# Down projection of a GeGLU feed-forward: product M2 moved between the groups of a half, and W21 loaded once per half

## The chip, the cores and the metric

The kernel runs on one core of a Trainium2 chip. The metric is the device time of one execution in microseconds (us), as the median over several runs. A core has a matrix engine (TensorE, "PE" in the profile, with its weight loads as "PEld"), three engines for elementwise work (VectorE or DVE, ScalarE or ACT, GpSimd or POOL), and SyncE (SP), which here issues most of the DMAs. The engines run side by side, each works through its own instructions in order, and they wait for each other on semaphores. TensorE writes its results to PSUM, eight banks of 128 x 512 f32, numbered 0 to 7.

## What is computed

```python
# x: (1, 2048, 1024), w_gate and w_up: (1024, 3584), w_down: (3584, 1024), all bf16
def reference(x, w_gate, w_up, w_down):
    return (_gelu(x @ w_gate) * (x @ w_up)) @ w_down
```

## The kernel before

The 2048 tokens are done in two halves (`h`) of 1024. For each half a gate/up part makes the hidden values `hT` (features on the partitions), and a down part multiplies them by `w_down`. The change lies in the down part, and this section tells of that.

**The seven products.** The down part works on two groups (`grp`) of 512 tokens per half, in `down_group`. In each group the product is split two by two, into blocks of 256 tokens, 1792 features and 512 output columns, and Strassen's scheme in Winograd's form makes it out of seven block products in place of eight. With A for the hidden values and W for `w_down`:

- S1 = A21 + A22, S2 = S1 - A11, S3 = A11 - A21, S4 = A12 - S2
- T1 = W12 - W11, T2 = W22 - T1, T3 = W22 - W12, T4 = W21 - T2
- M1 = A11 W11, M2 = A12 W21, M3 = S4 W22, M4 = A22 T4, M5 = S1 T1, M6 = S2 T2, M7 = S3 T3
- C11 = M1 + M2, C22 = M1 + M6 + M7 + M5, C12 = M1 + M6 + M5 + M3, C21 = M1 + M6 + M7 + M4

M1 and M2 take bf16 operands as they are. The other five take sums, kept in f32 form (`s_mem` for S and the copy of A22, `t_mem` for T and the copy of W22). A product is 14 steps (`NS`, 128 features each) for each of two sets of 128 tokens (`u`), so 28 matmuls of 128 x 512, which `product` issues in a list's order.

**The banks.** Each product has a pair of banks, one for each `u`. M1 goes to PB and is copied to QB by ScalarE (L781). M5 goes to VB and is copied out to `m5` (L802). M6 is added to QB, which is then copied to RB (L817), and `add_m5` adds M5 to QB on VectorE (L742). M7 is added to RB, and a second `add_m5` writes RB + M5 to VB, which is C22. M2 is added to PB (C11), M3 to QB (C12), M4 to RB (C21). `evacuate` (L766 and L768, in halves L757 and L759) casts finished banks to bf16 in `o_sb` buffers, of which there are four, and `store` (L774) sends them out from SyncE. PB, VB, QB and RB are the pairs (0, 1), (2, 3), (4, 5), (6, 7).

**The order.** It is written out by hand: `pe`, `dve`, `act` and `sp` chain an engine's instructions in the order in which the program issues them. In a group it is M1, M5, M6, M7, M2, M3, M4. The `behind_...` functions put the work for later products between the matmuls of the running one: S by `s_down` on VectorE (L675; the copy of A22 on ScalarE, L667), T1 and T3 by `t_down` on VectorE (L605), the copy of W22 on ScalarE (L602), T2 and T4 by DMA from a DRAM buffer, `t_dram`, that the first half's gate/up part filled (L600). `t_mem` is a ring of 20 blocks for five sequences of 14, so a T load waits for the matmuls that read the block before. In the first half, X for the next half is loaded from DRAM during the first group's M6 and M7 (L973, behind `x_fill`).

**W21.** `load_b21` (L569) loads it in four tiles: three of 512 KB into `wd_sb` buffers, of which there are three, and the last of 256 KB into an `o_sb` buffer. Each group issues all four behind M6. In a half's first group one of the three `wd_sb` buffers still holds a part of S3 that M7 reads.

Of the kernel before, what the change touches and what calls it, by code (L numbers as in the profile page):

```python
# [34 lines left out]
def kernel(  # L35
# [33 lines left out]
    NS = KF // 2  # L69
    NR = 20  # L70
    NGRP = SH // TB
# [35 lines left out]
    PB, VB, QB, RB = (0, 1), (2, 3), (4, 5), (6, 7)  # L107
# [11 lines left out]
    def sp(inst):  # L119
        return on("sp", inst)  # L120

    def act(inst):
        return on("act", inst)

    def dve(inst):
        return on("dve", inst)
# [12 lines left out]
    def pe(inst):  # L139
        return on("pe", inst)  # L140
# [414 lines left out]


    BPT = WDT * D // DN
    b21_tiles = {}

    def load_b21(n, q):  # L560
        i0, i1 = q * BPT, min((q + 1) * BPT, NS)
        if i1 < NS:
            w = wd_pool.tile([P, WDT, D], BF16, name="wd_sb")
            w = w[:].rearrange("p a d -> p (a d)")
        else:
            w = o_pool.tile([P, (i1 - i0) * DN], BF16, name="o_sb")[:]
        w = w.rearrange("p (b n) -> p b n", n=DN)
        src = wdv[:, NS + i0 : NS + i1, 0:DN]
        sp(nc.sync.dma_start(out=w[:, 0 : i1 - i0, :], in_=src))  # L569
        b21_tiles[(n, q)] = w  # L570

    def right(grp, name, i0, i1):

# [18 lines left out]
    def t_down(grp, name, i0, i1):  # L592

        for i in range(i0, i1, 2):
            t = right(grp, name, i, i + 2)
            rows = wd_rows(i, i + 2)
            b11, b12 = rows[:, :, 0:DN], rows[:, :, DN:D]
            if name in ("t2", "t4"):
                src = t_dram[:, i : i + 2, 0 if name == "t2" else 1, :]
                sp(nc.sync.dma_start(out=t.bitcast(F32), in_=src))  # L600
            elif name == "b22":
                act(nc.scalar.copy(out=t, in_=b22_blocks(i, i + 2)))  # L602
            else:
                in0, in1 = (b12, b11) if name == "t1" else (b22_blocks(i, i + 2), b12)
                dve(nc.vector.tensor_tensor(out=t, in0=in0, in1=in1, op=ALU.subtract))  # L605
# [51 lines left out]
    def s_down(hT, grp, name, i0, i1):  # L657
        n = 0 if name in ("s1", "s2", "s4") else 1
        for i in range(i0, i1, 2):
            t = s3_early(i) if (grp, name) == (0, "s3") and i < 4 else left(n, i, i + 2)  # L660

            def a(l, j):
                c0 = grp * TB + l * 2 * P
                return hT[:, j * NS + i : j * NS + i + 2, c0 : c0 + 2 * P]

            if name == "a22":
                act(nc.scalar.copy(out=t, in_=a(1, 1)))  # L667
                continue
            in0, in1, op = {
                "s1": lambda: (a(1, 0), a(1, 1), ALU.add),  # L670
                "s2": lambda: (t.bitcast(F32), a(0, 0), ALU.subtract),
                "s3": lambda: (a(0, 0), a(1, 0), ALU.subtract),
                "s4": lambda: (a(0, 1), t.bitcast(F32), ALU.subtract),
            }[name]()
            dve(nc.vector.tensor_tensor(out=t, in0=in0, in1=in1, op=op))  # L675
# [2 lines left out]
    NSPLIT = 4  # L678
    DH = DN // 2

    def down_group(hT, h, grp, then):
        last_grp = h == NH - 1 and grp == NGRP - 1
        more = grp + 1 < NGRP
        t0 = grp * TB
        n = h * NGRP + grp

        def done(name):
            for f in then.get(name, ()):
                f()
# [7 lines left out]
        def product(name, bset, lhs, rhs, start, stop, behind=None, order=plain):  # L697

            left_of = [0] * NS
            for i, u, *part in order:  # L700
                bank, c0, c1 = part or (bset[u], 0, DN)
                pe(
                    nc.tensor.matmul(  # L703
                        banks[bank][:, c0:c1],
                        lhsT=lhs(i, u),
                        rhs=rhs(i)[:, c0:c1],
                        start=start and i == 0,
                        stop=stop and i == NS - 1,
                        skip_group_check=True,
                    )  # L710
                )
                left_of[i] += 1
                if behind is not None and left_of[i] == 2 and i % 2 == 1:
                    behind(i - 1)

        def h_block(l, j):
            def lhs(i, u):
                c0 = t0 + (2 * l + u) * P
                return hT[:, j * NS + i, c0 : c0 + P]

            return lhs

        def lsum(n):
            return lambda i, u: left(n, i, i + 1)[:, 0, u * P : (u + 1) * P]
# [6 lines left out]
        def rsum(name):  # L731
            return lambda i: right(grp, name, i, i + 1)[:, 0, :]
# [2 lines left out]
            return wd_rows(i, i + 1)[:, 0, 0:DN]  # L735

        def b21(i):
            return b21_tiles[(h * NGRP + grp, i // BPT)][:, i % BPT, :]

        def add_m5(dst, src, u):  # L740
            dve(
# [5 lines left out]
        def evacuate(bset, l, d, halves=False):  # L747

            outs = []
            for u in range(2):  # L750
                if halves and u == 1:
                    r0 = h * SH + t0 + (2 * l + u) * P
                    for bank, c in ((bset[u], 0), (VB[u], DH)):
                        dst = o_pool.tile([P, DN], BF16, name="o_sb")[:, 0:DH]
                        src = banks[bank][:, c : c + DH]
                        if c == 0:
                            dve(nc.vector.tensor_copy(out=dst, in_=src))  # L757
                        else:
                            act(nc.scalar.copy(out=dst, in_=src))  # L759
                        c0 = d * DN + c  # L760
                        outs.append((out2[r0 : r0 + P, c0 : c0 + DH], dst))
                    continue
                dst = o_pool.tile([P, DN], BF16, name="o_sb")[:]
                r0 = h * SH + t0 + (2 * l + u) * P
                if last_grp and u == 0:
                    dve(nc.vector.tensor_copy(out=dst, in_=banks[bset[u]][:]))  # L766
                else:
                    act(nc.scalar.copy(out=dst, in_=banks[bset[u]][:]))  # L768
                outs.append((out2[r0 : r0 + P, d * DN : (d + 1) * DN], dst))
            return outs  # L770

        def store(outs):
            for dst, src in outs:
                sp(nc.sync.dma_start(out=dst, in_=src))  # L774

        def store_last(dst, src):
            act(nc.scalar.dma_start(out=dst, in_=src))

        product("m1", PB, h_block(0, 0), b11, True, False)
        for u in range(2):  # L780
            act(nc.scalar.copy(out=banks[QB[u]][:], in_=banks[PB[u]][:]))  # L781
        done("m1")

        def behind_m5(i):

            s_down(hT, grp, "s2", i, i + 2)
            if NT2 + i < NS:
                t_down(grp, "t2", NT2 + i, NT2 + i + 2)
            elif more:
                late.append(i + NT2 - NS)  # L790
            else:
                t_down(grp, "t3", i + NT2 - NS, i + NT2 - NS + 2)
# [12 lines left out]
        def behind_m6(i):  # L805
            if NT2 + i < NS:
                t_down(grp, "t3", NT2 + i, NT2 + i + 2)
            else:
                s_down(hT, grp, "s4", i + NT2 - NS, i + NT2 - NS + 2)
            if i == 4:  # L810
                for q in range(4):
                    load_b21(n, q)

        product("m6", QB, lsum(0), rsum("t2"), False, False, behind_m6, tail)
        s_down(hT, grp, "s4", NT2, NS)
        for u in range(2):
# [14 lines left out]
        s_down(hT, grp, "a22", 0, NS)  # L831
        out22 = evacuate(VB, 1, 1)
        done("m7")
        store(out22)
        product("m2", PB, h_block(0, 1), b21, False, True)
        out11 = evacuate(PB, 0, 0)
        done("m2")


# [6 lines left out]
                    t_down(grp + 1, "t1", NT2 + i - NS, NT2 + i - NS + 2)  # L846

        product("m3", QB, lsum(0), rsum("b22"), False, True, behind_m3)
        store(out11 + evacuate(QB, 0, 1))
        done("m3")  # L850

        def behind_m4(i):
            if not more:
                return
            if NT2 + i < NS:
                t_down(grp + 1, "t1", NT2 + i, NT2 + i + 2)
            else:
                t_down(grp + 1, "t2", NT2 + i - NS, NT2 + i - NS + 2)
# [23 lines left out]
    for h in range(NH):  # L882
# [9 lines left out]
        for pair in range(first_pair, NPAIR):  # L892
# [14 lines left out]
            if h == 0 and pair >= PPG:  # L907

                n = [min(4 * (pair - PPG + d), NSTEP) for d in range(3)]
# [16 lines left out]
            if 6 < pair < 11:  # L926
                i = 2 * pair - 8
# [81 lines left out]
        for grp, then in enumerate((then0, then1)):  # L1009
            down_group(hT, h, grp, then)  # L1010
# [30 lines left out]
```

## Time and profile before

| | |
|---|---|
| time of 3 runs, median | 539.78 us |
| lowest and highest | 539.51 and 540.17 us |
| span of the profiled execution, first to last instruction | 538.0 us |
| granted TensorE clock over the span | 1.000 |
| down groups within the span | 183.2 to 271.3 us, 447.0 to 535.1 us |
| DMA: moved, mean rate | 102.70 MB, 191 GB/s |

The profile is of one execution, whose own time is told by its span; the runs' times are of executions without a profile and hold some 1.8 us around the span as well. Busy times are of instructions, without waits. A row of the timeline has the start in us from the span's start, the length in us, the engine, the line of the kernel, the operation, out<-in, and how many instructions it merges; what stands in brackets is the engine's idle time before it and what ended it. Some matmul records are missing from the trace, so a product of 28 shows 27 at times. Rows of DMA queues (SPq) show the issue alone; the time to the landing is asked for by tile or line.

### The profile page before, as it was taken

How to read it: one execution, taken by the hardware profiler on the slowest of the kernel's cores; microseconds unless marked ns; L12 is line 12 of the kernel's file. 1: busy time of each engine (PE TensorE's matmuls, PEld its weight loads, DVE VectorE, ACT ScalarE, POOL GpSimd, SP SyncE). 2: the span in 40 equal slices, each digit the busy share in tenths (PEclk: the TensorE clock that was granted, in tenths of full speed). 3: DMA queues.
4: the chain of work that ended last, by engine and by line, in shares of the span. 5: the costliest groups of instructions: out<-in, count | busy, mean ns of one | idle time of the engine just before them, and what ended most of it. 6: DMA issues, size and time to landing. Idle time of an engine off the chain costs nothing.

```text
span 538.0 us, 7084 instructions
## 1 busy us (share of the span) xinstructions
PE 532.4 (99%) x2352; PEld 377.9 (70%) x2388; DVE 364.2 (68%) x476; ACT 263.5 (49%) x447; POOL 244.4 (45%) x212
## 2 busy tenths in 40 slices
PE   9999999999999999999999999999999999999997
PEld 4577776666776686777776677777777766866866
DVE  1988777788775997989574334444444469969861
ACT  2555555555555329117465555555555552462280
POOL 0699877777776000000056776666777730000000
PEclk9999999999999999999999999999999999999999
DMA  9946876785815977789950405041322448677846
GB/s 205 323 128 195 207 252 185 238 262 197 291 61 200 361 239 246 237 279 308 324 171 1 156 1 158 15 142 57 100 78 80 155 133 284 220 246 252 293 141 212
DMA packets 92547, 102.70 MB, mean 191 GB/s; under 512 B 18656, under 2 KB 67424, under 8 KB 92512
## 3 DMA queue, kind: packets, MB, share of 16 engines
q1 hardware_dynamic: 69568, 80.23, 46.0%
q10 hardware_dynamic: 22944, 22.02, 13.4%
q8 instruction: 19, 0.31, 0.2%
q14 instruction: 16, 0.13, 0.1%
HBM read 85.98 MB, written 12.58 MB: 183 GB/s over the span
## 4 chain that ended last, share of the span: by engine, by line
PE 99%; issue 0%; ACT 0%; ACTq 0%
PE bank L413 63%; PE bank L703 33%; PE bank L264 3%; PE bank L202 1%; PE bank L308 0%; ACT bank L468 0%; ACT o_sb L759 0%; ACTq L468 0%
## 5 line engine op out<-in xcount | busy, mean ns | idle before, releaser
L413 PE MATMUL bank<-t_mem,s_mem 128*128 128x512 f32 x1056 | 249.6, 394 | 0.0
L413 PEld LDWEIGHTS bank<-t_mem,s_mem 128*128 128x128 f32 x1056 | 198.1, 188 | 44.1 <-DVE bank L436 0.4
L385 POOL TENSOR_TENSOR s_mem<-w_mem 128x512 fp32r<-128x512 bf16 x102 | 120.3, 1201 | 190.7 <-DVE t_mem L259 102.8
L703 PE MATMUL bank<-t_mem,s_mem 128*128 128x512 f32 (+1 forms) x548 | 127.2, 391 | 0.0
L288 DVE TENSOR_TENSOR hT<-w_mem,bank 128x512 bf16<-128x512 f32 x104 | 71.3, 687 | 79.9 <-PE bank L413 45.7
L703 PEld LDWEIGHTS bank<-t_mem,s_mem 128*128 128x128 f32 x548 | 102.4, 188 | 22.1 <-issue 0.2
L436 DVE TENSOR_TENSOR bank<-bank,m 128x512 f32<-128x512 f32 x108 | 69.9, 694 | 45.2 <-ACT m L458 43.7
L413 PE MATMUL bank<-xT,w_mem 128*128 128x512 bf16 x405 | 96.5, 380 | 1.4
L283 ACT ACTIVATE w_mem<-bank 128x512 f32<-128x512 f32 x104 | 61.8, 596 | 52.9 <-DVE bank L436 35.8
L413 PEld LDWEIGHTS <-w_mem 128*128 128x128 bf16 x432 | 40.2, 98 | 51.6 <-issue 6.8
L385 POOL TENSOR_TENSOR s_mem<-w_mem,s_mem 128x512 fp32r<-128x512 bf16 x52 | 65.8, 1285 | 0.0
L605 DVE TENSOR_TENSOR t_mem<-w_mem 128x1024 fp32r<-128x1024 bf16 x56 | 65.6, 1219 | 0.0
L385 POOL TENSOR_TENSOR s_mem<-s_mem,w_mem 128x512 fp32r<-128x512 f32 x52 | 60.9, 1192 | 0.0
L464 ACT COPY bank<-bank 128x512 f32<-128x512 f32 x54 | 30.8, 570 | 38.9 <-PE bank L413 38.9
L398 ACT CAST s_mem<-w_mem 128x512 fp32r<-128x512 bf16 x54 | 33.1, 615 | 30.6 <-PE bank L413 29.1
L675 DVE TENSOR_TENSOR s_mem<-hT 128x512 fp32r<-128x512 bf16 x52 | 34.2, 686 | 10.2 <-PE bank L703 9.4
L458 ACT COPY m<-bank 128x512 f32<-128x512 f32 x54 | 31.8, 589 | 17.5 <-PE bank L413 17.5
L703 PEld LDWEIGHTS <-hT 128*128 128x128 bf16 x224 | 21.3, 98 | 26.6 <-issue 2.1
L468 ACT COPY bank<-bank 128x512 f32<-128x512 f32 x54 | 30.7, 570 | 12.7 <-PE bank L413 12.7
L630 DVE TENSOR_TENSOR o_sb<-wd_sb,o_sb 128x512 fp32r<-128x512 bf16 x28 | 31.5, 1126 | 0.5
L768 ACT CAST o_sb<-bank 128x512 bf16<-128x512 f32 x27 | 14.8, 585 | 33.9 <-PE bank L703 33.9
L602 ACT CAST t_mem<-w_mem 128x1024 fp32r<-128x1024 bf16 x28 | 26.9, 1048 | 0.0
(45 smaller groups left out, 238.6 us busy)
## 6 DMA issues: line engine op xcount, KB each, us to landing
t_mem<-t_dram SPq DMA_DIRECT2D x56, 512.0 KB, 5.2
w_mem<-in_w_gate_dram ACTq DMA_DIRECT2D x10, 1024.0 KB, 5.5
w_mem<-in_w_up_dram ACTq DMA_DIRECT2D x10, 1024.0 KB, 5.5
wd_sb<-in_w_down_dram SPq DMA_DIRECT2D x28, 256.0 KB, 4.5
t_dram<-o_sb SPq DMA_DIRECT2D x28, 256.0 KB, 2.4
wd_sb<-in_w_down_dram SPq DMA_DIRECT2D x12, 512.0 KB, 7.7
w_mem<-in_w_down_dram SPq DMA_DIRECT2D x4, 1024.0 KB, 6.6
w_mem<-in_w_down_dram SPq DMA_DIRECT2D x8, 512.0 KB, 8.3
```

What stands on the lines that cost most here:

```text
L283: act(nc.scalar.activation(out=g_sb, in_=ps[:], func=ACT.Gelu_apprx_tanh))
L288: nc.vector.tensor_tensor(out=hT[:, fc, tb * TB : (tb + 1) * TB], in0=g_sb, in1=ps[:], op=ALU.mult,)
L385: pool(nc.gpsimd.tensor_tensor(out=t, in0=in0, in1=in1, op=op))
L398: act(nc.scalar.copy(out=t, in_=a(1, 1)))
L413: nc.tensor.matmul(banks[bank][:], lhsT=lhs[:, c, :], rhs=rhs[:, c, :], start=start and c == 0, stop=c == KH - 1, skip_group_check=True,)
L436: nc.vector.tensor_tensor(out=banks[dst][:], in0=banks[src][:], in1=m5[j][:], op=ALU.add)
L458: act(nc.scalar.copy(out=m5[j][:], in_=banks[V_[j]][:]))
L464: act(nc.scalar.copy(out=banks[RB[j]][:], in_=banks[QB[j]][:]))
L605: dve(nc.vector.tensor_tensor(out=t, in0=in0, in1=in1, op=ALU.subtract))
L630: dve(nc.vector.tensor_tensor(out=t, in0=in0, in1=in1, op=ALU.subtract))
L675: dve(nc.vector.tensor_tensor(out=t, in0=in0, in1=in1, op=op))
L703: nc.tensor.matmul(banks[bank][:, c0:c1], lhsT=lhs(i, u), rhs=rhs(i)[:, c0:c1], start=start and i == 0, stop=stop and i == NS - 1, skip_gr ...
```

## The change

In a half's first group M2 is no longer done after M7. It is held back (`held`) and done at the start of the second group, ahead of that group's M1. In the second group of the first half M2 stays between M7 and M3. In the last group of all it follows M1 at once. The order of products is then:

| group | before | after |
|---|---|---|
| first of each half | M1 M5 M6 M7 M2 M3 M4 | M1 M5 M6 M7 M3 M4 |
| second, first half | M1 M5 M6 M7 M2 M3 M4 | held M2, M1 M5 M6 M7 M2 M3 M4 |
| second, second half | M1 M5 M6 M7 M2 M3 M4 | held M2, M1 M2 M5 M6 M7 M3 M4 |

The three large tiles of W21 are loaded once per half, behind the first group's M6, and kept for both M2. The small fourth tile is loaded for each group: behind M3 in a first group, behind M6 in the second group of the first half, and behind M1 in the last group. The second group of a half swaps the bank pairs PB and VB. Where no M2 stands between M7 and M3, M7's outputs are stored together with M3's.

```diff
     BPT = WDT * D // DN
+    NQ21 = -(-NS // BPT)
...
-        b21_tiles[(n, q)] = w
+        b21_tiles[(n if i1 == NS else n // NGRP, q)] = w
...
+    held = []
+
     def down_group(hT, h, grp, then):
+        PB, VB = ((0, 1), (2, 3)) if grp == 0 else ((2, 3), (0, 1))
...
-            return b21_tiles[(h * NGRP + grp, i // BPT)][:, i % BPT, :]
+            q = i // BPT
+            return b21_tiles[(n if q == NQ21 - 1 else h, q)][:, i % BPT, :]
...
+        def m2():
+            product("m2", PB, h_block(0, 1), b21, False, True)
+            return evacuate(PB, 0, 0)
+
+        if held:
+            store(held.pop()())
         product("m1", PB, h_block(0, 0), b11, True, False)
         for u in range(2):
             act(nc.scalar.copy(out=banks[QB[u]][:], in_=banks[PB[u]][:]))
         done("m1")
+        if last_grp:
+            load_b21(n, NQ21 - 1)
+            store(m2())
...
-            if i == 4:
-                for q in range(4):
+            if i == 4 and not last_grp:
+                for q in range(NQ21 - 1) if more else (NQ21 - 1,):
                     load_b21(n, q)
...
         out22 = evacuate(VB, 1, 1)
         done("m7")
-        store(out22)
-        product("m2", PB, h_block(0, 1), b21, False, True)
-        out11 = evacuate(PB, 0, 0)
+        if not more and not last_grp:
+            store(out22)
+            out22 = m2()
         done("m2")
...
-        store(out11 + evacuate(QB, 0, 1))
+        store(out22 + evacuate(QB, 0, 1))
         done("m3")
+        if more:
+            load_b21(n, NQ21 - 1)
+            held.append(m2)
```

## The prediction

> **What bounds the kernel now.** I read the busy times and the chain that ended last first. TensorE is busy 99% of the span and the chain runs through it almost alone. So the kernel gains only by shorter TensorE work, and loses whatever makes TensorE wait.
>
> ```profile
> PE 532.4 (99%) x2352; PEld 377.9 (70%) x2388; DVE 364.2 (68%) x476; ACT 263.5 (49%) x447; POOL 244.4 (45%) x212
> ...
> PE 99%; issue 0%; ACT 0%; ACTq 0%
> ```
>
> Then I cut the four down groups (two halves, two groups each) out of the span.
>
> ```profile
> core 0: us, PE busy (x) PEld busy (x) DVE busy (x) ACT busy (x) POOL busy (x), PEclk, DMA share, GB/s
> 183.20:227.20 44.00, 43.90 (x195) 31.54 (x196) 39.30 (x49) 17.25 (x27) 0.00 (x0) 1.00 0.75 260
> 227.20:271.30 44.10, 43.99 (x196) 31.73 (x198) 35.92 (x44) 20.90 (x34) 0.00 (x0) 1.00 0.91 299
> 447.00:491.00 44.00, 43.89 (x196) 31.66 (x198) 39.30 (x49) 17.25 (x27) 0.00 (x0) 1.00 0.71 237
> 491.00:535.10 44.10, 43.99 (x199) 31.91 (x200) 28.16 (x39) 16.15 (x25) 0.00 (x0) 1.00 0.70 233
> ```
>
> A group is 196 matmuls: 140 in f32, one every 226.7 ns in steady state, and 56 in bf16, one every 215.8 ns. That makes 43.8 us, and 44.0 to 44.1 are spent: there is no stall to win. But VectorE is busy 39.3 of 44 us in the first groups, so the question is what it still owes when M2 is no longer between M7 and M3. The timeline around that M2 answers it (start, length, engine, line).
>
> ```profile
> 200.51 4.63 DVE L605 TENSOR_TENSOR t_mem<-w_mem 128x1024 fp32r<-128x1024 bf16 x4
> ...
> 205.05 4.30 DVE L675 TENSOR_TENSOR s_mem<-hT,s_mem 128x512 fp32r<-128x512 bf16 x7
> ...
> 208.39 5.35 PE L703 MATMUL bank<-wd_sb,hT 128*128 128x512 bf16 x23
> 209.27 2.49 DVE L742 TENSOR_TENSOR bank<-bank,m 128x512 f32<-128x512 f32 x4
> ...
> 213.58 1.03 PE L703 MATMUL bank<-o_sb,hT 128*128 128x512 bf16 x4
> ```
>
> M7 ends and M2 (the two bf16 rows) begins at 208.39. VectorE, without a pause, makes T3 (L605), S4 (L675) and only then, from 209.27, the four adds of M5 (L742). The first two of these write QB, the banks that M3 goes on adding to. They are late by more than 2 us, and M2's 5.9 us hide that.
>
> **The change, part by part.** The order of VectorE's instructions does not change: after the seven S4 come the two QB adds, then M3 may start.
>
> *M3 straight behind M7, first group of each half.* The adds stand 0.60 us apart and take 0.69 each: QB0 is ready at 209.27 + 0.69 = 209.96, QB1 at 209.87 + 0.69 = 210.56. What TensorE does after such a wait is seen once in this trace, in the gate/up part:
>
> ```profile
> 29.83 1.28 DVE L436 TENSOR_TENSOR bank<-bank,m 128x512 f32<-128x512 f32 x2
> ...
> 30.57 0.76 PEld L413 LDWEIGHTS bank<-t_mem,s_mem 128*128 128x128 f32 x4 [0.40 <-DVE bank L436]
> ```
>
> The first add ended at 30.52, the waiting weight load started 0.05 later, and the matmul after the released one started at 30.91, that is 0.39 after the add. M3's second matmul waits for QB1, so its third starts at 210.56 + 0.39 = 210.95. Without a wait it would start at 208.39 + 2 x 0.227 = 208.84. Loss 2.11 us (1.94 if only the second matmul's slot counts). The second half has the same rows (M2 at 472.16, adds from 473.03, so QB1 at 474.32): 2.11 again. Sum 4.2 us.
>
> *M3 straight behind M7, last group.* There T3 is spread over M5 and M6, and VectorE is less late:
>
> ```profile
> 490.96 6.22 PE L703 MATMUL bank<-w_mem,hT 128*128 128x512 bf16 x27
> ...
> 497.05 1.06 ACT L781 COPY bank<-bank 128x512 f32<-128x512 f32 x2 [5.27 <-PE bank L703]
> ...
> 515.77 2.49 DVE L742 TENSOR_TENSOR bank<-bank,m 128x512 f32<-128x512 f32 x4
> 516.10 5.35 PE L703 MATMUL bank<-wd_sb,hT 128*128 128x512 bf16 x23
> ```
>
> QB1 is ready at 516.37 + 0.69 = 517.06, the third matmul starts at 517.45 instead of 516.55: 0.90 us (0.73 the other way). VectorE's lateness is set by M5's progress in this group, not by M1, so the M2 put in front of M5 does not help it; M2's own evacuation on VectorE (0.69) fits before the first S2, which waits 1.3 us into M5.
>
> *M2 straight behind M1, last group.* M2 adds to the PB banks that the L781 copies still read (M1 is kept in QB too). They run from 497.05 to 498.11 because M1's results end there. Today M5, in other banks, covers them. M1 starts at 490.96, its 28 slots (28 x 0.2158, and 0.02 for the turn from f32) end at 497.02, and M2's second matmul, due at 497.24, waits for 498.11 + 0.05: 0.92 us (0.6 if only the first copy held it, 1.1 with a slow restart). In the second group of both halves the held M2 stands before M1, and their banks are different pairs after the swap of PB and VB, so M1 doesn't wait for M2's evacuation.
>
> *Fewer turns between bf16 and f32.* Today M1 and M2 are eight bf16 islands; after it five. An island costs little: from M7's last start (208.16) to M3's eleventh (216.76) are 8.60 us, and 0.23 + 28 x 0.2158 + 10 x 0.2267 is 8.54. Three islands fewer give 3 x 0.06 = 0.19 us (0.3 by the groups' surplus over 43.8; nothing where the restarts above take its place).
>
> *T4 in the first half.* M4 now starts 3.7 us earlier: M3's third matmul at 210.95 puts M4's start at 216.86. Its T4 blocks come by DMA (L600): three loads behind M7, four paced by M3. The last four move with M3, but the queue before them is full. Asked for one by one, issue plus time to landing, it went so: third W21 tile landed at 207.9, fourth 209.5, X for the next half 211.7 and 213.1, T4 215.9, 217.2 and 218.5, two stores by 219.2, T4 again 220.5 to 225.4. The last one landed just as M4 wanted it (22nd matmul, 225.4). The new deadline is 216.86 + 21 x 0.227 = 221.6. Ahead of it the fourth W21 tile (1.61) and the stores (0.70) are gone: 225.4 - 2.3 = 223.1, 1.5 us late. If the steps that took 2 to 3 us were bubbles, all at the best pace of 1.3 give 213.1 - 1.6 + 7 x 1.3 = 220.6, and the one slow step that each run of four loads shows (2.4 instead of 1.3) makes 221.7, 0.1 late. I take the middle of 0.1 and 1.5, 0.8, ends 0 and 2. In the second half X is not loaded, the four loads took 8.8 us from an idle queue, the deadline is 9.8 after the first issue: nothing. In the last group likewise.
>
> *W21 once per half.* Two sets of three 512 KB loads leave; they were issued in M6 and due after M7, so nothing. The fourth tile (256 KB) moves behind M3's stores and must wait for the first of them to land, some 223.5 in the first half; today's four such loads took 4.2 to 9.7 us from issue to landing, and the 25th matmul of the held M2 wants the tile at about 229.3. That is nothing by the short rows and up to 3.9 by the longest, which stood in the queue behind three other W21 loads. I take nothing, because here only stores stand before it. Queued behind it on SyncE are T2 loads that M6 wants 15 us later and two stores. M7's stores move behind M3: ScalarE has evacuated by then, and the buffer that they free later is the one just priced. The held M2's stores sit on SyncE in front of T2's second part until ScalarE has evacuated, 1.3 us into M1: M1 and M5 cover that.
>
> *Sum.* 2.11 + 2.11 + 0.90 + 0.92 + 0.8 - 0.19 = 6.65 us. The span is 538.0, the runs' median 539.8; the 1.8 between lie outside the program's instructions and stay. The time predicted is 539.8 + 6.65 = 546.4.
>
> *Does the clock hold?* The granted clock is 1.00 in all four groups, where TensorE never pauses; the only slow matmuls are the seven warm-up ones, 0.45 us apart in the first 4 us. So a 2 us pause is not shown by this trace. If each of the two long ones cost another 4 us at half speed, that is 2 x 2 = 4 us more.
>
> The Trainium skill ("TensorE: Matmul & The Clock Gate", Part 1) halves the clock only after an idle window of about 3.4 us, and no run here shows it; by that rule these pauses of 2 us would cost nothing more.
>
> **The rivals.**
> - *The pauses don't come (539.6).* If VectorE gave the QB adds before M7's end, only the islands would count, 0.19 us. That is decided at 208.39 against 210.56: something would have to free 2.2 us of VectorE's 4.30 for S4 before it. VectorE has no gap from 183 to 211.8 and its order is unchanged, which speaks against it. Chance 0.05, for the time being equal or better.
> - *DMA counts in full (548.5).* T4 late by 2 in the first half and the fourth W21 tile by about 1: 546.4 + 1.2 + 0.9. For it: the queue is full from 206 to 224. Chance 0.09.
> - *The clock drops (550.4).* As priced above. Chance 0.04.
>
> **How the numbers follow.** My forecast has the other 0.82. Its own ends: 1.94 x 2 + 0.73 + 0.8 - 0.3 = 5.1 without any DMA wait, 544.9; and 2.2 x 2 + 1.0 + 1.0 + 2.0 = 8.4, 548.2. To hold 8 in 10, I give 544.7 to 548.6. About 0.2% (1.1 us) is what a measurement of this kernel can tell from no change; faster by more 0.02, within 0.03, slower by more 0.95.
>
> **What would show it.** Right: in both first groups M3's first weight load with about 1.6 us idle before it, released by VectorE's add, and a second short wait; about 0.4 plus 0.6 in the last group; in its M2 a wait on ScalarE's copy; in the first half's M4 a wait of under 1.6 us on T4's DMA. Wrong: M3 following M7 without idle time, a granted clock under 1.00 behind a pause, or a wait in a held M2.

## The result, and the profile after

The change made the kernel slower: 546.88 us median (546.30 to 547.33, 4 runs) against 539.68 us (539.51 to 540.17, 4 runs of before beside them). The ratio is 1.0131, with a 95% interval of 1.0119 to 1.0144. The forecast was 546.4, within 544.7 to 548.6. The profiled execution of after took 546.49 us, and its span is 544.7 us, 6.6 more than before. The medians are 7.2 apart, mostly because this execution lies 0.4 below the median of after.

First the busy times and the chain that ended last, of after:

```profile
PE 536.5 (98%) x2388; PEld 377.7 (69%) x2388; DVE 364.2 (67%) x476; ACT 263.5 (48%) x447; POOL 244.1 (45%) x212
...
PE 4%; DVE 2%; issue 1%; ACT 0%
```

The other engines did the same work in the same time as before. (PE's busy time is 4.1 higher although its matmuls are the same: 36 more of their records are in this trace.) The chain, 99% PE before, is followed back through PE and then VectorE for a few per cent of the span only: VectorE is now on the path. The waits of TensorE, with what ended them, in total, times and longest:

```profile
PE bank L707 <- ACT s_mem L668: 1.6, 1, 1.6
PE bank L707 <- DVE bank L747: 1.1, 2, 0.8
...
PE bank L707 <- DMA t_mem<-t_dram: 0.5, 1, 0.5
...
PE bank L707 <- ACT bank L792: 0.4, 1, 0.4
```

Before, there was no such row for the down part. Below, a pause is counted as in the prediction, by what the distance between two matmul starts has over its usual 0.227 (f32) or 0.216 us (bf16); the view counts less, because its idle time starts only at the modelled end of the matmul before.

From the start of M1 to the end of the part, the first half's down part took 90.21 us instead of 87.93, so 2.28 more. The second half's, with the end of the kernel, took 94.99 instead of 91.02, so 3.97 more. The gate/up part between them took 175.84 both times. What is left of the 6.64 is 0.39 us ahead of the first down part, which the change does not touch.

The timeline of after at M3 of the first group (start, length, engine, line) shows the biggest pause:

```profile
206.64 3.09 DVE L676 TENSOR_TENSOR s_mem<-hT,s_mem 128x512 fp32r<-128x512 bf16 x5
206.73 2.20 PE L707 MATMUL bank<-t_mem,s_mem 128*128 128x512 f32 x9
...
209.65 2.49 DVE L747 TENSOR_TENSOR bank<-bank,m 128x512 f32<-128x512 f32 x4
209.74 2.70 ACT L668 CAST s_mem<-hT 128x512 fp32r<-128x512 bf16 x5
210.46 0.19 PEld L707 LDWEIGHTS bank<-t_mem,s_mem 128*128 128x128 f32 x1 [1.95 <-ACT s_mem L668]
210.49 1.72 PE L707 MATMUL bank<-t_mem,s_mem 128*128 128x512 f32 x5 [1.56 <-ACT s_mem L668]
211.00 1.01 PEld L707 LDWEIGHTS bank<-t_mem,s_mem 128*128 128x128 f32 x5 [0.35 <-DVE bank L747]
```

M7 ends, TensorE stops, VectorE finishes S4 (L676) and begins the adds (L747) at 209.65. The first add ends at 209.65 + 0.69 = 210.34, and M3's waiting weight load starts at 210.46. The second ends at 210.94, and the next waiting weight load starts at 211.00. One row names ScalarE's copy of A22 as the releaser, although M3 does not read A22. The times fit VectorE's add better, and the first experiment decides it.

The other pauses, from the same view: M4's wait in the first half (as the weight load shows it), a T2 load in M6 of the second half, M3 behind it, M2 behind M1 in the last group, and M3 there.

```profile
222.13 1.45 PEld L707 LDWEIGHTS bank<-t_mem,s_mem 128*128 128x128 f32 x7 [0.34 <-issue]
...
467.58 1.83 PE L707 MATMUL bank<-t_mem,s_mem 128*128 128x512 f32 x7 [0.53 <-DMA t_mem<-t_dram]
...
476.54 1.23 PE L707 MATMUL bank<-t_mem,s_mem 128*128 128x512 f32 x3 [0.78 <-DVE bank L747]
...
501.76 1.06 ACT L792 COPY bank<-bank 128x512 f32<-128x512 f32 x2 [2.76 <-PE bank L707]
502.38 0.87 PE L707 MATMUL bank<-wd_sb,hT 128*128 128x512 bf16 x2 [0.44 <-ACT bank L792]
...
528.27 1.93 PE L707 MATMUL bank<-t_mem,s_mem 128*128 128x512 f32 x6 [0.35 <-DVE bank L747]
```

By the starts of the matmuls: M3 in the first half lost 2.11 us and M4's wait for T4 there 0.19; the second half's M6 lost 0.77 and its M3 1.34, together 2.11; M2 behind M1 lost 0.88; M3 of the last group 0.90. That is 6.19 us of pauses, 2.30 in the first half and 3.89 in the second.

### The profile page after: what moved, and what is told of

Its sections match the earlier page's. It is cut to its first block, busy times and chain, and to the rows that moved or that the text cites. A ratio compares the mean times of both kernels' runs of the same rounds, so it can differ in the third digit from the quotient of the medians.

```text
span 544.7 us, 7109 instructions
## 1 busy us (share of the span) xinstructions
PE 536.5 (98%) x2388; PEld 377.7 (69%) x2388; DVE 364.2 (67%) x476; ACT 263.5 (48%) x447; POOL 244.1 (45%) x212
## 5 line engine op out<-in xcount | busy, mean ns | idle before, releaser
L385 POOL TENSOR_TENSOR s_mem<-w_mem 128x512 fp32r<-128x512 bf16 x102 | 119.1, 1188 | 193.7 <-DVE t_mem L259 105.0
L413 PE MATMUL bank<-xT,w_mem 128*128 128x512 bf16 x432 | 98.0, 380 | 0.0
L676 DVE TENSOR_TENSOR s_mem<-hT 128x512 fp32r<-128x512 bf16 x52 | 34.2, 686 | 2.5 <-PE bank L707 1.7
```

The source lines that it names most:

```text
L385: pool(nc.gpsimd.tensor_tensor(out=t, in0=in0, in1=in1, op=op))
L413: nc.tensor.matmul(banks[bank][:], lhsT=lhs[:, c, :], rhs=rhs[:, c, :], start=start and c == 0, stop=c == KH - 1, skip_group_check=True,)
```

## The experiments

Three theories had to be told apart for the pause at M3: VectorE's late adds (the forecast), ScalarE's copies (which one row names), or something that comes with M3 behind M7 whatever the engines do. After that came the question of what M2 had covered besides, and whether anything is to be had from the change.

**1. The adds ahead of the last S4.** To after:

```diff
-        s_down(hT, grp, "s4", NT2, NS)
         for u in range(2):
             act(nc.scalar.copy(out=banks[RB[u]][:], in_=banks[QB[u]][:]))
             add_m5(QB[u], QB[u], u)
+        s_down(hT, grp, "s4", NT2, NS)
```

> The changed kernel, with one move on VectorE in every group: the two M5 adds to QB go ahead of the last four S4 instead of behind them. Theory V (M3 waits for VectorE's QB adds): QB1 is ready 4 x 0.60 = 2.4 us earlier, so M3 follows M7 without a wait in all three places: minus 2.11, 2.11 and 0.90. M1 to M2 in the last group (0.88) stays. M4 of the first half's first group starts 2.1 us earlier, and the T4 loads before it are bound by the DMA queue, so its wait grows from 0.2 to about 1.5 to 2.1. Time 546.9 - 5.1 + 1.6 = 543.4 (543.1 to 543.8). Theory S (M3 waits for ScalarE, which the trace names in one row as releaser, its copies of A22 and W22): nothing changes for ScalarE, time 546.9.

Measured: 544.41 us (543.89 to 545.83), ratio to before 1.0087 (1.0068 to 1.0106). No pause at M3 is left in any group, with ScalarE's copies where they were: the releaser in after was VectorE, and the ScalarE row is a misattribution. But only about 2.5 us came back, of the 5.1 that M3 (with M6 of the second half) had lost. The timeline and the windows of this kernel show why:

```profile
204.69 13.99 PE L707 MATMUL bank<-t_mem,s_mem 128*128 128x512 f32 x61
219.72 0.70 PE L707 MATMUL bank<-t_mem,s_mem 128*128 128x512 f32 x2 [1.04 <-DMA t_mem<-t_dram]
221.00 2.51 PE L707 MATMUL bank<-t_mem,s_mem 128*128 128x512 f32 x7 [0.57 <-DMA t_mem<-t_dram]
```

M4 now waits for its T4 loads: 2.1 us in the first half by the matmul starts, and 0.88 in the second, which the expected time did not have. The pause at M3 in after had given those loads 2.1 us more, so the two costs lay over each other. And the clock, which had held in after's profile, fell in this execution (mean 0.997; the other three runs show 1.000). The windows have the start and end, the length, each engine's busy time, and then PEclk, the granted clock:

```profile
core 0: us, PE busy (x) PEld busy (x) DVE busy (x) ACT busy (x) POOL busy (x), PEclk, DMA share, GB/s
218.54:221.95 3.41, 1.80 (x7) 1.15 (x7) 3.41 (x4) 0.17 (x1) 0.00 (x0) 1.00 0.64 225
221.95:225.36 3.41, 3.17 (x8) 1.44 (x9) 3.41 (x6) 1.00 (x2) 0.00 (x0) 0.50 0.79 249
225.36:228.77 3.41, 3.41 (x17) 1.57 (x16) 2.23 (x4) 0.00 (x0) 0.00 (x0) 1.00 0.93 313
```

After the two waits the clock stood at 0.50 for 3.41 us, with matmuls 0.427 us apart, and was whole again.

**2. The last group's M2 back between M7 and M3**, the held M2 as in after:

```diff
-        if last_grp:
-            load_b21(n, NQ21 - 1)
-            store(m2())
...
-            if i == 4 and not last_grp:
+            if i == 4:
...
-        if not more and not last_grp:
+        if not more:
```

> The changed kernel, but in the last group M2 stands between M7 and M3 again; only the held M2 of the two first groups is left of the move. Theory V: the last group's two waits (0.88 for M2 behind M1's copies, 0.90 for M3 behind the QB adds) go, one more turn between bf16 and f32 comes (0.06): 546.9 - 1.7 = 545.2. If the last group's waits only stood in for a later one (the final stores), less is gained: 546 to 546.9.

Measured: 544.65 us (543.41 to 545.70), ratio 1.0087 (1.0065 to 1.0108). Both first groups pause 2.11 us at M3, and the last group not at all.

**3. Nothing held:** M2 of the first groups where it was before, and M1, M2 together in the last group.

```diff
-        if held:
-            store(held.pop()())
...
-                for q in range(NQ21 - 1) if more else (NQ21 - 1,):
+                for q in range(NQ21) if more else (NQ21 - 1,):
...
-        if not more and not last_grp:
+        if not last_grp:
...
-        if more:
-            load_b21(n, NQ21 - 1)
-            held.append(m2)
```

> The changed kernel, but no M2 is held: both groups of the first half and the first group of the second have M2 between M7 and M3 as before; M2 directly behind M1 in the last group and W21 once per half stay. Theory V: only the last group's two waits are left, 539.7 + 0.88 + 0.90 - 0.06 = 541.4. With the run of the last group as before, the two parts must add up to the whole: 545.2 + 541.4 - 539.7 = 546.9.

Measured: 541.95 us (541.80 to 542.62), ratio 1.0040 (1.0025 to 1.0055). The down parts have two pauses only, 0.88 us behind M1 and 0.90 ahead of M3, both in the last group. The two halves of the change add up: 1.0087 x 1.0040 = 1.0127, against 1.0131 for the whole.

**4. The order of before, W21 loaded once per half:** the edits of 2 and 3 together.

> Order of the products as before the change; only the three large W21 tiles are loaded once per half (and the banks of the second group are swapped). Theory V: nothing of it is on the path, 539.7 (539.5 to 540.0). Rival W (the fewer loads pay, by T4 and T2 coming sooner): 539.0 to 539.4.

Measured: 539.96 us (539.58 to 540.30), ratio 1.0000 (0.9991 to 1.0010). The loads that leave were not on the path.

**5. X later.** To experiment 1, X for the next half goes out behind M4 instead of behind M6 and M7, so that it does not stand ahead of T4:

```diff
-            then0["m6"] = [x_fill]
+            then0["m4"] = [x_fill]
```

> The kernel with the QB adds ahead of the last four S4, and the two loads of X for the next half moved from M6 to M4 of the first group. Theory Q (with M3 no longer late, M4 waits for T4 because the DMA queue is full of X ahead of it): the waits in the first half's M4 fall from 2.1 us to what the second half, which loads no X there, showed (0.8 in its M4), and so does the half-speed clock window behind them (1.7): 544.4 - 1.3 = 543.1 against its median, 542.5 if no run has the slow window. If T4's landing is set by M3's progress and not by the queue, the wait stays: 544.4.

Measured: 543.69 us (542.69 to 544.21), ratio 1.0063 (1.0045 to 1.0081), not to be told from experiment 1 by the intervals. M4 of the first half still waits 1.6 us for T4, and of the second 0.8, where X had never been. X was not most of it.

**6. The third W21 tile later as well,** behind M3 in the first groups:

```diff
-                for q in range(NQ21 - 1) if more else (NQ21 - 1,):
+                for q in range(NQ21 - 2) if more else (NQ21 - 1,):
...
         if more:
+            load_b21(n, NQ21 - 2)
             load_b21(n, NQ21 - 1)
```

> The same, and the third W21 tile, which the held M2 does not need before M4's end, is loaded behind M3 with the fourth instead of in front of T4. Theory Q: nothing stands before T4 in the queue, its seven loads land in time in both halves; left is the last group's wait of M2 for M1's copies (0.88): 540.0 + 0.88 - 0.19 = 540.7. If T4 is late by M3's pace: 542 to 543.

Measured: 542.66 us (542.18 to 543.46), ratio 1.0051 (1.0035 to 1.0066). M4 waits 1.3 us in the first half and 0.9 in the second, though neither X nor W21 stands in the queue ahead of T4 any more. What is left is the series itself: its seven loads are issued some 0.9 us apart, from 206.68 to 212.16, and land 1.3 to 2.4 us apart, from 210.24 to 220.45. The last four, issued from 209.44 on, so take 11 us from the first issue to the last landing. With M4 straight behind M3 that is not soon enough.

**7. M1 and M2 of the last group one bank after the other.** To experiment 6, all 14 matmuls of `u` = 0 come ahead of those of `u` = 1 in both products:

```diff
+        by_u = [(i, u) for u in range(2) for i in range(NS)]
+        m12 = by_u if last_grp else plain
...
-            product("m2", PB, h_block(0, 1), b21, False, True)
+            product("m2", PB, h_block(0, 1), b21, False, True, None, m12)
...
-        product("m1", PB, h_block(0, 0), b11, True, False)
+        product("m1", PB, h_block(0, 0), b11, True, False, None, m12)
```

> The same, and in the last group M1 and M2 run through one set of 128 tokens (u) after the other, so that ScalarE copies M1's first bank while the second is still being made. Theory V: the last wait goes, all cover is back, and only the three fewer turns between bf16 and f32 are left: 539.97 - 0.19 = 539.8 (539.4 to 540.2), as long as the kernel before. If M2 waits for the fourth W21 tile instead, which is now needed 2.6 us into M2: 540.3 to 541.

Measured: 541.41 us (540.72 to 542.47), ratio 1.0028 (1.0019 to 1.0037). The timeline of its M1 and M2 has no wait:

```profile
492.56 6.21 PE L707 MATMUL bank<-w_mem,hT 128*128 128x512 bf16 x27
498.60 2.75 PE L707 MATMUL bank<-wd_sb,hT 128*128 128x512 bf16 x12
```

The copy of bank 0 ran while M1 filled bank 1, and the copy of bank 1 while M2 added to bank 0. The expected time assumed that the T loads would come in time, and they didn't: T4 cost 0.73 us in the first half's first group, 0.41 in the second half's, 0.18 and 0.12 in the groups behind them, and T2 0.34 in the first half's second group. That is 1.78 us, and the span is 1.8 longer than before's.

**8. The adds made later.** To after, two more adds on VectorE in front of each QB add, in the first groups; they write VB, whose contents are overwritten later:

```diff
+            if more:
+                for _ in range(2):
+                    dve(
+                        nc.vector.tensor_tensor(
+                            out=banks[VB[u]][:], in0=m5[u][:], in1=m5[u][:], op=ALU.add
+                        )
+                    )
             add_m5(QB[u], QB[u], u)
```

> The changed kernel with two idle additions on VectorE (their result is overwritten) ahead of each QB add in the two first groups: QB1 is ready 4 x 0.60 = 2.4 us later. Theory V (VectorE's lateness goes one for one into the time): 546.9 + 2 x 2.4 - 0.2 = 551.5 if the granted clock holds. Theory C (the clock halves for one window of 3.4 us when more than about half of a window is idle, as the kernel with the early adds showed at 1.95 us idle): pauses of 4.5 us cost 1.7 to 3.4 more each: 555 to 558. Theory S (M3 waits for ScalarE): 546.9.

Measured: 555.74 us (554.74 to 558.10), ratio 1.0298 (1.0273 to 1.0322), 8.9 us over after. By its first two intervals (the third already runs at half clock) the pause at M3 is 4.67 us in the first half and 4.65 in the second; by the same two it is 2.00 in after's first half and in both halves of experiment 2, which has no wait in M6. So it grew by 2.67 and 2.65 us. The second QB add ended 2.67 and 2.65 us later as well, counted from M7's last start. That accounts for 5.3 of the 8.9. Most of the rest goes with the clock: its mean is 0.987 to 0.991 in the four runs, against 0.997 to 1.000 in after's. The timeline and the windows of this kernel (the execution with the profile, at 558.10 us, is the slowest of the four, and also has a wait of 1.1 us in the gate/up part):

```profile
213.53 0.47 PE L707 MATMUL bank<-t_mem,s_mem 128*128 128x512 f32 x1 [2.90 <-DVE bank L747]
215.37 9.00 PE L707 MATMUL bank<-t_mem,s_mem 128*128 128x512 f32 x26 [1.37 <-DVE bank L747]
```

```profile
211.15:214.56 3.41, 0.47 (x1) 0.19 (x1) 3.34 (x6) 3.41 (x8) 0.00 (x0) 1.00 0.97 347
214.56:217.97 3.41, 2.60 (x6) 2.12 (x7) 2.65 (x5) 1.79 (x4) 0.00 (x0) 0.50 0.64 246
217.97:221.39 3.42, 3.42 (x9) 2.64 (x9) 1.38 (x2) 0.00 (x0) 0.00 (x0) 0.50 0.80 238
221.39:224.80 3.41, 3.41 (x16) 2.79 (x16) 2.68 (x4) 0.39 (x1) 0.00 (x0) 1.00 0.88 258
```

After a window with one matmul in it the clock is 0.50 for two windows, 6.8 us, in which 15 matmuls start instead of some 30. The second half has such a stretch from 484.21 to 491.04, behind a window with five matmuls. So VectorE's adds set the pause, microsecond for microsecond, and a pause twice as long cost more than its length.

**9. M2 between M3 and M4 in the first groups.** To experiment 1, with the last group as in 7; X stays where before has it:

```diff
-        if held:
-            store(held.pop()())
...
-                for q in range(NQ21 - 1) if more else (NQ21 - 1,):
+                for q in range(NQ21) if more else (NQ21 - 1,):
...
-            load_b21(n, NQ21 - 1)
-            held.append(m2)
+            store(m2())
```

> Edit: the QB adds go ahead of the last four S4 as in e1; the first group's M2 stands between M3 and M4 instead of behind M4 (so all four W21 tiles are again loaded behind its M6); in the last group M1 and M2 run u by u as in e7. X stays behind M6 and M7. Theory (M2 did two jobs where it stood: it covered VectorE's late adds ahead of M3, and it gave the T4 loads 5.9 us more before M4; the first job can be done by an earlier add, the second by M2 anywhere ahead of M4): no wait in M3, no wait in M4, none between M1 and M2, a clock of 1.00, the time of before less up to 0.1 us for the islands: 539.7 (539.3 to 540.2). Rival D (what makes T4 late is the series of loads itself, paced by M3 and stretched by the queue, so that M2 behind M3 doesn't help): 0.5 to 2.5 us of waits in M4 in each half as in e1 and e7, 541 to 544. Rival V (M3 straight behind M7 costs even with the early adds): 0.3 us or more of waits at M3 in three groups, over 540.6.

Measured: 540.38 us (539.75 to 540.87, 11 runs) against 539.68 (539.21 to 540.68, 15 runs), ratio 1.0010 (1.0001 to 1.0019). The timeline around that M2 runs through from M7 (its start lies in the first row) to M4:

```profile
204.69 10.13 PE L707 MATMUL bank<-t_mem,s_mem 128*128 128x512 f32 x44
214.67 5.35 PE L707 MATMUL bank<-wd_sb,hT 128*128 128x512 bf16 x24
219.86 1.03 PE L707 MATMUL bank<-o_sb,hT 128*128 128x512 bf16 x4
220.53 1.75 PE L707 MATMUL bank<-t_mem,s_mem 128*128 128x512 f32 x6
```

Neither first group waits at M3 or in M4: once the adds are early, M2 covers T4 behind M3 as well as it did ahead of it. The expected time was just missed. The spans differ by 0.9 us, and the trace has 0.83 us of waits for T4: 0.35 in the first half's second group, where the last load landed at 269.62 instead of 268.43, and 0.48 in the last group, whose M4 no longer has an M2 in front of it.

No version was faster than before, which is also what its profile says: TensorE has nothing to wait for there.

## Why the prediction was right

- *What bounds the kernel.* Right. Nothing that the change frees was on the path (experiment 4), and every pause that it adds counts in full in the span: 6.19 us of pauses and 0.39 ahead of the down part are 6.58 of the 6.64 that the span grew.
- *M3 in the first groups, 2.11 each.* Right. The first half lost 2.11, and M3's third matmul starts 0.39 us behind the second add's end, as forecast. In the second half a T2 load landed late (467.45, with gaps of 2.65 and 2.94 us in its series against 1.24 in the quickest) and took 0.77 us in M6. That looks like chance: experiment 2, with the same order up to there, has no such wait. The delay cost nothing extra: VectorE's adds came 26.0 us after M1 as before, so M3 waited 1.34 instead of 2.11. While VectorE sets M3's start, a TensorE delay ahead of it is free. Experiments 1 and 8 show the cause in both directions.
- *M3 in the last group, 0.90, and M2 behind M1, 0.92.* Right: 0.90 and 0.88, by the matmuls' starts. Experiment 3 has both alone (1.78 us of pauses in a median 2.0 us longer), and 7 takes the second away.
- *T4 in the first half, 0.8.* This is the term that was mis-sized: 0.19 us. The loads came near the quick end of its bounds, so the bubbles of before were mostly not repeated: the last one landed at 222.02, which is 221.63 in the prediction's count (this execution reaches the down part 0.39 later), between its 220.6 and 223.1. Its deadline of 221.6 is the start of the 22nd matmul; what waits is that matmul's weight load, some 0.2 ahead, and so 221.63 cost 0.19. (M4 starts 4.0 us earlier than before, 220.87 to 216.86; the prediction's 3.7 is a slip that enters nothing.) The mechanism was real and sat just behind the pause: experiment 1 uncovers it at 2.1 us, and then it also appears in the second half, where the prediction had it at nothing with 1 us to spare. In after's second half it had about 0.1: the four loads took 9.7 us, not 8.8.
- *The fourth W21 tile and the stores, nothing.* Right: the tile was issued at 222.47, landed at 225.17, and the held M2 had no wait.
- *The islands (the turns between bf16 and f32), 0.19 won.* Not found. The pauses explain 2.30 of the first half's 2.28 and 3.89 of the second's 3.97, so what remains is between -0.02 and +0.08, and no run isolates it.
- *The clock.* It held at 1.00 in the profile of after, as taken, but the reason given for it fails. The Trainium skill ("TensorE: Matmul & The Clock Gate", Part 1) asks for an idle window of about 3.4 us. In experiment 1 the clock halved behind a window of 3.41 us in which seven matmuls ran, and in experiment 8 behind windows with one and with five. That the drop lasts whole windows of that length agrees with the page; that the window must be idle does not. What decided it in these runs was how much of a pause fell into one window. The changes of the granted clock within a trace lie whole multiples of 3.413 us apart: in experiment 1 at 221.95, 225.36 and, after the last matmul, 542.80 (1 and 93 windows); in experiment 8 at 214.56, 221.39, 484.21, 491.04 and 555.89. In after the clock falls after the last matmul, at 544.01; 98 and 99 windows back from there are 209.51 and 206.09, and that boundary cuts the long pause in two:

```profile
206.09:209.51 3.42, 2.84 (x13) 2.03 (x11) 3.42 (x7) 3.42 (x4) 0.00 (x0) 1.00 0.99 331
209.51:212.92 3.41, 2.39 (x9) 1.79 (x10) 3.22 (x6) 3.41 (x8) 0.00 (x0) 1.00 1.06 381
```

By the matmul starts, 0.73 us of pauses lie in the first of these windows and 1.38 in the second. In experiment 2 the same pauses are cut into 0.63 and 1.47, and 0.85 and 1.25, and the clock held. In experiment 1, 2.08 us fell into one window, in experiment 8 3.19 and 2.45, and there it halved. So in after's profile the clock held by luck, by where the windows lay: no trace here has a pause of 2.1 us inside one window of the running kernel that left the clock whole. One of the other runs of after has a mean clock of 0.997, and 0.3% of its 545.5 us is about what one window at half speed takes, 1.7 us; yet at 547.28 us it is no longer than the run with 1.000 (547.33). So the rival "the clock drops" was less remote than its 0.04 says, but at 1.7 for each of the two long pauses its price would have been 3.4 us, not 4.
- *The size of the whole.* 546.4 against 546.88: T4 was put 0.6 too high, while 0.2 was taken off for the islands and 0.39 came ahead of the down part in that execution. These offset each other by luck, so that the span grew by 6.64 against 6.65 forecast; the pauses other than T4's were right to 0.04 us.

## What to carry to other kernels

Before moving a piece of work that has no dependence on its neighbours, list what it covers where it stands: here M2 hid VectorE's backlog ahead of M3 and, unseen behind that, gave four DMA loads 6 us more before M4. Covers overlap, so that taking one wait away (experiment 1) may only show the next, and what ending one pause brings can be well under its length (2.5 of 5.1 us there). And where an engine must reload a bank that another still copies, ordering the matmuls bank by bank (experiment 7) hides the copy without any new buffer.

## What was not expected of the hardware

- The granted clock can halve after pauses that add up to about 2.1 us, with matmuls between them (experiment 1), though 2.11 us of pauses in after and in experiment 2 left it at 1.00 in the profile. The difference is the grid of 3.413 us windows: up to 1.47 us of pauses in one window between products left the clock whole in these traces, and 2.08 and more halved it for the next. Where between them the limit lies, no experiment settles.
- How long it stays at half goes with the slow window itself: it was whole again behind slow windows in which TensorE was busy for 3.17 us (experiment 1) and 3.42 (experiment 8), and stayed at half behind those with 2.60 us (experiment 8, first half) and 1.75 (second half).
- Four 512 KB loads issued 0.9 us apart took 8.8 us from the first issue to the last landing out of an idle queue (before's second half), and 11 us behind the first three loads of their own series (experiment 6). Single steps between landings were 1.2 to 2.9 us in one kernel (after), so a load that lands with less than some 2 us to spare will at times be late.
